# A state-space and feed-forward kernel: kernel products in steps of 48 matmuls, and an empty step behind inverse rows

## The chip, the cores and the metric

The kernel runs on one core of a Trainium2 chip. The metric is the device time in microseconds; the median of the runs shown is 1351.43 us. Beside it stands one profiled execution, which took 1350.32 us, with a span of 1348.5 us from its first to its last instruction.

## What is computed

One block with adaptive layer norm, for 2048 tokens of width 576: a state-space convolution (S4D), then a feed-forward network, both with a residual, in float32. Cut to what matters:

```python
def conv(u, ...):                        # _A_ref
    K = 2.0 * einsum("dn,dnl->dl", C, exp(A * dt * pos)).real
    y = irfft(rfft(u, 2 * L) * rfft(K, 2 * L))[:L]
    return y + u * D_skip
def ffn(x, w1, w2):                      # _B_ref, Dff = 4608
    return maximum(x @ w1, 0) @ w2

h = layernorm(x) * (1 + ca) + sa         # ca, sa, ga, ... from silu(c) @ w_mod
x = x + ga * conv(h)
h = layernorm(x) * (1 + cb) + sb
x = x + gb * ffn(h)
```

## The kernel before

The 2048 tokens are cut into four blocks of 512. The convolution is done blockwise by transforms of 1024 points that are written as matrix products and butterflies; block s needs the spectra of the inputs of all blocks up to s and those of the convolution kernel K.

K comes from products of power tables, `W2` (32 rows for each of 48 channels) and `W1`. A *head* h is 48 channels; there are twelve. For a stretch of K the tables of a head are rotated on VectorE (`rot`, lines 404 to 416: two multiplications with 1536 elements, two additions with 768), and then multiplied on TensorE (`products`, line 440): for each of 12 values q, for real and imaginary part, four 32-row matmuls that lie beside each other in the array. The result of six q, a *half* of 48 matmuls, fills the one PSUM buffer of the tag `cps`, and ScalarE copies it out (line 450). The first part of K is made before the feed-forward stage starts (`KGen`, line 262). The rest is made beside it by `rest`, with three widths: na = 48 columns (parts 1 to 3 together) and na = 16 (part 1 alone) in block 0, na = 32 (parts 2 and 3) in block 1.

The feed-forward stage fills most of the time. For each of 4 x 36 *groups* g of 128 hidden columns, `first(g)` makes 14 matmuls into `hps` (line 1326; float32 as a sum of high and low parts `xh`, `xl`, `xs`), ScalarE writes `hh` (line 1331) and VectorE `hl` (line 1332) out of it, and `second(g - 2)` makes 14 more into five accumulators `acc` (line 1351). There are two `hps` buffers. The weights `w` are loaded, split on ScalarE (lines 1297, 1304) and VectorE, and their low parts kept in HBM for the later blocks.

While block s is in the feed-forward stage, the *side work* for block s + 1 is woven in. It is a chain of Python generators (`gens`): in block 0 `rest` for the heads 0 to 5, then convolution 1; in block 1 the output of block 0 (`finish`), `rest` for the heads 6 to 11, then convolution 2; in block 2 convolution 3. Four times in each group `step` takes pieces from the chain. A piece of VectorE work yields its estimated microseconds; a piece of TensorE work yields `None`, which counts one of at most two such pieces for this step and 0.7 of credit; -1 ends the step. A step goes on while the credit is under its target, a rate times the step's number:

```python
            while done[0] < target and v < min(room, 2.7) and pe < 2:
                w = next(gen, 0)
                if gen.gi_frame is None or w == -1:
                    return
                if w is None:
                    pe += 1
                    done[0] += 0.7
```

At a block's end the rest of its chain is emitted at once. `spread` puts one yield of the products behind each rotation operation (behind each second one at na = 32, each third at na = 48). A recording layer then fixes each engine's order, so the order on an engine is not quite the order in which the code was emitted.

At the end of a convolution `inverse` makes four rows of tokens for each half of the channels: two matmuls into a `cps` buffer (line 1019), a yield of `None`, an addition to the residual x on VectorE (recorded by the helper `v`, line 510), a yield of 0.45. In blocks 1 to 3 there is one `cps` buffer, so a row's matmuls need the previous row's addition. Then follow the statistics of the next norm (`norm2`, BN_AGGR at line 819, the square root on ScalarE at line 820) and transposes (line 1070) into `xh`, `xl`, `xs` for the next block.

Of the kernel before, what the change touches and what calls it, by code (L numbers as in the profile page):

```python
# [46 lines left out]
class KGen:  # L47
# [335 lines left out]
    def rest(self, psum, items, beside=iter(())):  # L383
# [6 lines left out]
        with ExitStack() as ctx:  # L390
# [37 lines left out]
            def products(h, W1, W2, blocks):  # L428
                na = 16 * len(blocks)
                key = (h // 6, blocks)  # L430
                if key not in kes:
                    kes[key] = pt.tile([P, na, 72], F32, name=f"ker_{h}")
                ke = kes[key]
                for half in range(2):
                    ps = psum.tile([P, 6, na], F32, tag="cps", bufs=1, name="kps")
                    for q in range(6):
                        for r in range(2):
                            for dd in range(4):
                                ch = dd * 12 + 6 * half + q
                                nc.tensor.matmul(  # L440
                                    ps[32 * dd : 32 * dd + 32, q, :],
                                    W2[:, r, :, ch],
                                    W1[:, :na, r, ch],
                                    start=(r == 0),
                                    stop=(r == 1),
                                )
                        if q == 2:
                            yield None
                    q0 = 12 * (h % 6) + 6 * half
                    nc.scalar.activation(  # L450
                        ke[:, :, q0 : q0 + 6], ps.rearrange("p q a -> p a q"), AF.Copy
                    )
                    yield None
                rows[key] = rows.get(key, 0) + 1
                if rows[key] == 6:
                    yield -1
                    for i, s in enumerate(blocks):
                        self.store(
                            s, h // 6, ke[:, 16 * i : 16 * i + 16].rearrange("p a q -> p (a q)"),
                            nc.gpsimd,  # L460
                        )
# [5 lines left out]
            for i, (h, blocks) in enumerate(items):  # L467
                W2, W0, Z = nxt
                W1 = pt.tile([P, most, 2, H], F32, tag="W1", bufs=2, name=f"W1r_{h}")
                yield from spread(rots(W1, W0, Z, blocks), prev, len(blocks))  # L470
                if i + 1 < len(items):
                    nxt = load(items[i + 1][0])
                prev = products(h, W1, W2, blocks)
                if i + 2 == len(items):
                    yield next(beside, -1)
# [12 lines left out]
class Body:  # L488
# [381 lines left out]
    def conv(self, s):  # L870
# [4 lines left out]
        x2 = self.x2p[s % 2].tile([P, 4, D], F32, tag="x2", bufs=1, name=f"x2_{s}")  # L875
# [70 lines left out]

        def inverse(p, V):
            ops = lambda n2: [(self.gc[:, n2, c, :], V[:, n2, c]) for c in range(2)]
            return self.inverse(x2, p, ops)

        def back(p, Y):
            V = self.spec(f"V_{s}_{p}")
# [16 lines left out]
        else:  # L969
# [10 lines left out]
            yield from product(0, Y)  # L980
        yield from back(0, Y)
        yield from both(spec_K(1, ZK), after(3, inverse(0, Vs[0])))
        Y = self.spec(f"Y_{s}_1")
        yield from product(1, Y)
        yield from back(1, Y)
        yield -1
        yield -1
        yield from inverse(1, Vs[1])
        yield from self.norm2(s, x2, xp)

# [18 lines left out]
            v(y, y, T, op=op or ALU.add)  # L1009
            yield 1.35  # L1010

    def inverse(self, x2, p, ops, order=(0, 2, 1, 3)):

        xv = x2.rearrange("m n (dd p q) -> m n dd p q", dd=4, p=2)
        for n2 in order:
            ps = self.cps.tile([P, 512], F32, tag="cps", bufs=self.nps, name="ps_i")
            todo = ops(n2)
            for i, (a, b) in enumerate(todo):
                self.nc.tensor.matmul(  # L1019
                    ps[:, :PC], a, b, start=(i == 0), stop=(i == len(todo) - 1)  # L1020
                )
            yield None
            pv = ps[:, :PC].rearrange("m (dd q) -> m dd q", dd=4)
            self.v(xv[:, n2, :, p], pv, xv[:, n2, :, p], op=ALU.add)
            yield 0.45

    def norm2(self, s, x2, xp, st=None):

# [553 lines left out]
```

## Time and profile before

| | us |
|---|---|
| median of the runs | 1351.43 |
| fastest run | 1349.67 |
| profiled execution | 1350.32 |
| its span | 1348.5 |
| first to last FF matmul | 214.8 to 1342 |

Busy time by stage of this execution (the four blocks of the feed-forward stage begin at 214.8, 550.0, 846 and 1108 us):

| stretch, us | PE busy | DVE busy | ACT busy | PE clock | GB/s |
|---|---|---|---|---|---|
| 214.8 to 550 | 324.9 of 335.2 | 291.1 | 102.2 | 0.97 | 291 |
| 550 to 846 | 291.5 of 296.0 | 206.9 | 104.2 | 0.99 | 283 |
| 846 to 1107.8 | 261.1 of 261.8 | 163.1 | 96.1 | 1.00 | 247 |
| 1107.8 to 1342 | 234.2 of 234.2 | 30.2 | 69.9 | 1.00 | 177 |

How to read the lines: PE is TensorE, PEld its weight loads, DVE VectorE, ACT ScalarE, POOL GpSimd, SP SyncE. A row of the order in time gives the start in us, the busy time, engine, line, operation, tiles out<-in, and the number of merged instructions; in brackets stands the idle time before it and what ended it, "issue" where the profile shows nothing that was waited for. Matmuls overlap, so PE's busy time says little of how fast they follow each other: for that the starts are compared. A float32 product of line 440 or 1019 appears as two matmul records, an FF matmul or a transpose as one.

### The profile page before, as it was taken

What the parts mean: (1) busy time and instruction counts of PE and PEld (TensorE: products, weight loads), DVE (VectorE), ACT (ScalarE), POOL (GpSimd) and SP (SyncE); (2) the same over time, 40 slices, a digit from 0 to 9 for tenths busy, and PEclk for the clock granted to TensorE, in tenths of its full rate; (3) what the DMA queues carried; (4) which work ended last, traced back from release to release, by engine and by line L of the source; (5) the groups of instructions that cost most, each with busy time, mean ns of one, the idle gap of its engine ahead of it and who ended that gap; (6) DMA issues with size and microseconds to landing.
All of it is one profiled execution on the core that took longest, in us unless ns stands there. A gap on an engine that the chain in (4) does not pass through costs nothing. (4 is left out here: it accounts for less than half of the span.)

```text
span 1348.5 us, 26042 instructions
## 1 busy us (share of the span) xinstructions
PE 1227.2 (91%) x10608; PEld 974.3 (72%) x10608; DVE 870.4 (65%) x1351; ACT 504.1 (37%) x1014; POOL 195.6 (15%) x271
## 2 busy tenths in 40 slices
PE   5124798999999998999999899999999999999998
PEld 3123566777777787787777787787888888888886
DVE  5977998999886899379546976376989221111111
ACT  7986234222224322622233225343222353332321
POOL 1777331111121100111101000100010000000000
PEclk9555898999999998999999999999999999999999
DMA  6666399888798975699688895767997556666651
GB/s 197 239 254 230 110 366 376 329 297 297 264 340 278 328 266 183 213 395 338 228 280 302 289 351 162 247 187 260 321 345 239 175 178 217 194 197 201 194 170 62
DMA packets 132424, 340.47 MB, mean 252 GB/s; under 512 B 22352, under 2 KB 22672, under 8 KB 132304
## 3 DMA queue, kind: packets, MB, share of 16 engines
q1 hardware_dynamic: 105200, 215.21, 48.1%
q0 software_dynamic: 26816, 123.01, 25.0%
q8 instruction: 83, 1.36, 0.4%
q10 hardware_dynamic: 288, 0.59, 0.1%
q14 instruction: 37, 0.30, 0.1%
HBM read 258.55 MB, written 80.22 MB: 251 GB/s over the span
## 5 line engine op out<-in xcount | busy, mean ns | idle before, releaser
L1351 PE MATMUL acc<-hh,w 128*128 128x512 f32 x1296 | 422.6, 400 | 2.1 <-DVE w L510 2.0
L1326 PE MATMUL hps<-xh,w 128*128 128x512 f32 x1152 | 395.9, 404 | 1.2 <-ACT xh L1082 1.2
L1351 PEld LDWEIGHTS acc<-hh,w 128*128 128x128 f32 x1296 | 243.8, 189 | 55.6 <-DVE w L510 2.8
L1351 PE MATMUL acc<-hl,w 128*128 128x512 f32 x720 | 279.9, 399 | 0.0
L1332 DVE SCALAR_TENSOR_TENSOR hl<-hps,hh 128x512 fp32r<-128x512 f32 x144 | 99.3, 689 | 279.8 <-ACT hh L1331 279.6
L1326 PEld LDWEIGHTS hps<-xh,w 128*128 128x128 f32 x1152 | 217.2, 190 | 49.7 <-ACT xh L1082 3.3
L1326 PE MATMUL hps<-xl,w 128*128 128x512 f32 x576 | 231.1, 401 | 0.6 <-DVE xl L1087 0.6
L1331 ACT ACTIVATE hh<-hps 128x512 fp32r<-128x512 f32 x144 | 86.2, 598 | 343.9 <-PE hps L1326 335.7
L1304 ACT ACTIVATE w<-r 128x576 fp32r<-128x576 f32 x144 | 98.7, 686 | 237.3 <-issue 183.9
L1351 PEld LDWEIGHTS acc<-hl,w 128*128 128x128 f32 x720 | 135.8, 189 | 28.3
L1326 PEld LDWEIGHTS hps<-xl,w 128*128 128x128 f32 x576 | 109.2, 190 | 25.6 <-DVE xl L1087 2.2
L262 PE MATMUL kps<-W,W 128*32 128x16 f32 x2304 | 40.1, 218 | 74.4 <-POOL W L59 49.3
L1297 ACT ACTIVATE w<-r 128x640 fp32r<-128x640 f32 x142 | 103.9, 732 | 5.9 <-DMA r<-in_w_dram 5.9
L1326 PE MATMUL hps<-xs,w 128*128 128x512 f32 x288 | 98.2, 421 | 2.9 <-DVE hl L1332 2.7
L262 PEld LDWEIGHTS kps<-W,W 128*32 128x32 f32 x2304 | 37.7, 150 | 79.1 <-POOL W L59 50.7
L510 DVE TENSOR_TENSOR Y<-Y,T 128x1152 f32<-128x1152 f32 x64 | 85.0, 1356 | 0.1
L440 PEld LDWEIGHTS kps<-W1r,W2r 128*32 128x32 f32 x3456 | 64.4, 146 | 26.8 <-issue 20.2
L440 PE MATMUL kps<-W1r,W2r 128*32 128x48 f32 (+2 forms) x3456 | 73.4, 238 | 3.9 <-issue 3.9
L759 ACT ACTIVATE Z<-ps_f 128x288 f32<-128x288 f32 x104 | 42.4, 408 | 63.9 <-PE ps_f L758 62.9
L1326 PEld LDWEIGHTS hps<-xs,w 128*128 128x128 f32 x288 | 53.6, 192 | 16.0 <-DVE hl L1332 4.2
L510 DVE TENSOR_TENSOR W<-Z 128x576 f32<-128x576 f32 x52 | 37.1, 756 | 40.9 <-ACT Z L759 40.9
L510 DVE TENSOR_TENSOR w<-r,w 128x512 fp32r<-128x512 f32 (+2 forms) x108 | 58.4, 580 | 3.0 <-ACT w L1304 3.0
(216 smaller groups left out, 1370.1 us busy)
## 6 DMA issues: line engine op xcount, KB each, us to landing
r<-in_w_dram SPq DMA_DIRECT2D x144, 320.0 KB, 4.3
r<-in_w_dram SPq DMA_DIRECT2D x144, 288.0 KB, 3.9
w<-L1d SPq DMA_DIRECT2D x108, 320.0 KB, 3.0
w<-L2d SPq DMA_DIRECT2D x108, 288.0 KB, 3.1
W2r<-W2d POOLq DMA_DIRECT2D x18, 1536.0 KB, 10.0
W2d<-W SPq DMA_DIRECT2D x10, 1536.0 KB, 7.4
W<-W1d POOLq DMA_DIRECT2D x18, 768.0 KB, 9.1
Ua<-Ud POOLq DMA_DIRECT2D x12, 1152.0 KB, 10.0
```

What stands on the lines that cost most here:

```text
L262: self.nc.tensor.matmul(ps[32 * dd : 32 * dd + 32, 12 * u + q, :], W2[:, r, :, ch], W1[:, u, :, r, ch], start=(r == 0), stop=(r == 1),)
L440: nc.tensor.matmul(ps[32 * dd : 32 * dd + 32, q, :], W2[:, r, :, ch], W1[:, :na, r, ch], start=(r == 0), stop=(r == 1),)
L510: return self.kept(self.nc.vector.tensor_tensor(*args, **kw))
L759: nc.scalar.activation(Z[:, n2, c], ps[:, :PC], AF.Copy)
L1297: nc.scalar.activation(w[:, 0], r, AF.Copy)
L1304: nc.scalar.activation(w[:, 0:D], r2[g], AF.Copy)
L1326: nc.tensor.matmul(ps, a, x, start=(i == 0), stop=(i == 13))
L1331: nc.scalar.activation(hh, ps, AF.Relu)
L1332: nc.vector.scalar_tensor_tensor(hl, ps, 0.0, hh, op0=ALU.max, op1=ALU.subtract)
L1351: nc.tensor.matmul(acc[i], a, x, start=(f == 0 and j in (0, 3, 6, 9, 12)), stop=(f == NF - 1 and j in (2, 5, 8, 11, 13)),)
```

## The change

Two edits. In `products` the yield behind the third q of a half stays only at na = 48. At 16 and 32 columns a half is then one TensorE piece of 48 matmuls with 0.7 of credit, where it was two pieces of 24 with 1.4. In the convolutions 2 and 3 (s > 1) each row of `inverse` yields -1 behind its addition, which ends the step.

```diff
@@ -444,7 +444,7 @@
                                     stop=(r == 1),
                                 )
-                        if q == 2:
+                        if q == 2 and na == 48:
                             yield None
@@ -946,7 +946,7 @@
         def inverse(p, V):
             ops = lambda n2: [(self.gc[:, n2, c, :], V[:, n2, c]) for c in range(2)]
-            return self.inverse(x2, p, ops)
+            return self.inverse(x2, p, ops, spaced=s > 1)
@@ -1009,7 +1009,7 @@
-    def inverse(self, x2, p, ops, order=(0, 2, 1, 3)):
+    def inverse(self, x2, p, ops, order=(0, 2, 1, 3), spaced=False):
@@ -1023,6 +1023,8 @@
             self.v(xv[:, n2, :, p], pv, xv[:, n2, :, p], op=ALU.add)
             yield 0.45
+            if spaced:
+                yield -1
```

Lines behind 1023 stand two further on in the changed kernel (1326 is 1328 there). Both edits move the side work behind them, since the credit of a step decides how much of the chain the next one takes.

How the change moves instructions is shown at three places. On ScalarE, beside the last products of 32 columns in block 1 (`ker` is the copied half of K, `mv` the statistics of the next norm, `hh` and `w` the FF stage's), before:

```order
L450 ACTIVATE ker_6735<-kps 128x32x6
L820 ACTIVATE mv<-mv,eps 128x1 x4
L1304 ACTIVATE w_7329<-r_7072 128x576
L450 ACTIVATE ker_6735<-kps 128x32x6
L1331 ACTIVATE hh<-hps 128x512
L1297 ACTIVATE w_7354<-r_7325 128x640
```

and in the change:

```order
L1306 ACTIVATE w_7437<-r_7222 128x576
L820 ACTIVATE mv<-mv,eps 128x1 x2
L1333 ACTIVATE hh<-hps 128x512
L1299 ACTIVATE w_7460<-r_7433 128x640
L450 ACTIVATE ker_6735<-kps 128x32x6
L820 ACTIVATE mv<-mv,eps 128x1 x2
L450 ACTIVATE ker_6735<-kps 128x32x6
```

The four roots are two pairs now, and an eviction of products stands behind the first pair, with hh and a weight split between. On TensorE, the first products of 32 columns in block 1, before:

```order
L440 MATMUL kps<-W1r_6628,W2r_6566 32x32 x48
L1351 MATMUL acc_36_6515<-hh,w_6603 128x512 x2
L1351 MATMUL acc_36_6515<-hl,w_6603 128x512
L1351 MATMUL acc_36_6516<-hh,w_6603 128x512 x2
L1351 MATMUL acc_36_6516<-hl,w_6603 128x512
```

and in the change:

```order
L440 MATMUL kps<-W1r_6628,W2r_6566 32x32 x48
L1353 MATMUL acc_36_6515<-hh,w_6603 128x512 x2
L440 MATMUL kps<-W1r_6628,W2r_6566 32x32 x48
L1353 MATMUL acc_36_6515<-hl,w_6603 128x512
L1353 MATMUL acc_36_6516<-hh,w_6603 128x512 x2
```

The second half of the head follows behind two FF matmuls, where before its first 24 products came 14 FF matmuls after. On TensorE, the first inverse rows of convolution 2 in the change (those of before stand in the prediction):

```order
L1019 MATMUL ps_i<-V_0_8456,gc 128x288 x2
L1328 MATMUL hps<-xs_6142,w_8418 128x512 x2
L1328 MATMUL hps<-xh_6140,w_8418 128x512
L1328 MATMUL hps<-xl_6141,w_8418 128x512
L1328 MATMUL hps<-xh_6140,w_8418 128x512 x2
L1328 MATMUL hps<-xl_6141,w_8418 128x512
L1328 MATMUL hps<-xh_6140,w_8418 128x512 x2
L1328 MATMUL hps<-xl_6141,w_8418 128x512
L1328 MATMUL hps<-xh_6140,w_8418 128x512 x2
L1328 MATMUL hps<-xl_6141,w_8418 128x512
L1328 MATMUL hps<-xh_6140,w_8418 128x512
L1019 MATMUL ps_i<-V_0_8456,gc 128x288 x2
```

Fourteen FF matmuls lie between the first row and the second.

## Prediction

> **What bounds the kernel now.** I read the page first, then the busy time by stretches, then the order in time around groups of side work.
>
> ```profile
> span 1348.5 us, 26042 instructions
> PE 1227.2 (91%) x10608; PEld 974.3 (72%) x10608; DVE 870.4 (65%) x1351; ACT 504.1 (37%) x1014; POOL 195.6 (15%) x271
> q8 instruction: 83, 1.36, 0.4%
> L440 PE MATMUL kps<-W1r,W2r 128*32 128x48 f32 (+2 forms) x3456 | 73.4, 238 | 3.9 <-issue 3.9
> 1200.00:1300.00 100.00, 100.00 (x443) 82.81 (x442) 11.07 (x16) 30.62 (x48) 0.00 (x0) 1.00 0.64 196
> ```
>
> From 214.8 us to 1342 us TensorE hardly rests. Where it has feed-forward (FF) matmuls almost alone (the stretch row), 443 start in 100 us, 0.226 us each. So in these 1127 us everything else that PE does, and every wait of PE, adds to the end; the other engines count only where they make PE wait. Each convolution matmul has two records in the trace (1728 products of line 440 stand as 3456 records).
>
> **Part 1, fewer groups.** What does a cut in the products cost? Here is a step of 24 products (48 records) and one of two steps in a row:
>
> ```profile
> 599.79 0.39 PE L1326 MATMUL hps<-xh,w 128*128 128x512 f32 x1
> 600.11 0.94 PE L440 MATMUL kps<-W1r,W2r 128*32 128x32 f32 x48
> 600.98 0.73 PE L1351 MATMUL acc<-hh,w 128*128 128x512 f32 x2
> 601.55 0.39 PE L1351 MATMUL acc<-hl,w 128*128 128x512 f32 x1
> ...
> 631.57 0.39 PE L1351 MATMUL acc<-hl,w 128*128 128x512 f32 x1
> 631.89 1.65 PE L440 MATMUL kps<-W1r,W2r 128*32 128x32 f32 x96
> 633.47 0.72 PE L1326 MATMUL hps<-xs,w 128*128 128x512 f32 x2
> 634.03 0.40 PE L1326 MATMUL hps<-xh,w 128*128 128x512 f32 x1
> ```
>
> From FF matmul to FF matmul the 24 take 600.98 - 599.79 = 1.19 us, less 0.226 for the matmul itself 0.96, and the two matmuls behind take 0.57 instead of 0.45: 1.08 us. The 48 take 1.67 + 0.11 = 1.78 us. Two 24s cost 2.16, so a cut costs 0.38 us. In PE's order the groups of line 440 beside FF matmuls fall from 63 to 46 (32 columns 21 to 12, 16 columns 24 to 18, 48 columns 18 to 16): 17 x 0.38 = **-6.4 us**, the widths taken alike.
>
> **Part 2, what denser groups meet.** In the kernel-generation stage TensorE runs products without FF matmuls:
>
> ```profile
> 109.34 2.15 PE L262 MATMUL kps<-W,W 128*32 128x16 f32 x127 [1.42 <-issue]
> 113.30 2.15 PE L262 MATMUL kps<-W,W 128*32 128x16 f32 x128 [1.81 <-issue]
> 117.14 2.14 PE L262 MATMUL kps<-W,W 128*32 128x16 f32 x128 [1.70 <-issue]
> ```
>
> Runs of 127 or 128 records, each behind a wait for nothing that the profile shows. With their weight loads 128 records are 256 instructions, and the page has 83 packets on the instruction queue for PE's 2 x 10608: one packet per 256. I read the waits as the arrival of the next block of instructions. Blocks start 3.96 and 3.84 us apart though they run in 2.15. Beside FF matmuls (a block of them alone runs 128 x 0.226 = 29 us) this is hidden, except in two places, of which this is one:
>
> ```profile
> 252.83 1.51 PE L440 MATMUL kps<-W1r,W2r 128*32 128x16 f32 x88
> 254.27 0.73 PE L1326 MATMUL hps<-xs,w 128*128 128x512 f32 x2
> 254.93 0.90 PE L440 MATMUL kps<-W1r,W2r 128*32 128x16 f32 x48
> ...
> 257.12 0.54 PE L440 MATMUL kps<-W1r,W2r 128*32 128x16 f32 x20
> 259.44 0.66 PE L440 MATMUL kps<-W1r,W2r 128*32 128x16 f32 x28 [1.78 <-issue]
> 260.02 0.81 PE L1326 MATMUL hps<-xh,w 128*128 128x512 f32 x2
> ...
> 263.61 0.79 PE L1351 MATMUL acc<-hh,w 128*128 128x512 f32 x2
> 348.15 0.52 PE L440 MATMUL kps<-W1r,W2r 128*32 128x16 f32 x19 [1.65 <-issue]
> 259.40:348.10 88.70, 86.54 (x1405) 68.26 (x1405) 82.61 (x87) 21.18 (x39) 12.07 (x18) 0.98 0.86 297
> ```
>
> Between the two waits lie 1405 matmuls and as many weight loads, 2810 instructions, and 11 x 256 is 2816: both fall on a block's end (six waiting instructions are not counted as records). Counting 128 records back from 257.66, the block began near 253.4: it ran 4.2 us and waited 1.78, a turnaround of 6.0. Behind the wait nine FF matmuls take 263.61 - 260.02 = 3.59 us where 2.03 would do, at half speed: 1.6 us more. The two stalls cost 1.78 + 1.65 + 2 x 1.6 = 6.6 us.
>
> The change moves them. PE at the first stall, before (names: kps is the products' PSUM tile, hps and acc the two FF ones):
>
> ```order
> L440 MATMUL kps<-W1r_3032,W2r_3026 32x16 x44
> L1326 MATMUL hps<-xs_2779,w_3024 128x512 x2
> L440 MATMUL kps<-W1r_3032,W2r_3026 32x16 x24
> L1326 MATMUL hps<-xh_2777,w_3024 128x512
> L1326 MATMUL hps<-xl_2778,w_3024 128x512
> L1326 MATMUL hps<-xh_2777,w_3024 128x512 x2
> L1326 MATMUL hps<-xl_2778,w_3024 128x512
> L440 MATMUL kps<-W1r_3032,W2r_3026 32x16 x24
> ```
>
> and in the change:
>
> ```order
> L440 MATMUL kps<-W1r_3032,W2r_3026 32x16 x44
> L1328 MATMUL hps<-xs_2779,w_3024 128x512 x2
> L440 MATMUL kps<-W1r_3032,W2r_3026 32x16 x48
> L1328 MATMUL hps<-xh_2777,w_3024 128x512
> L1328 MATMUL hps<-xl_2778,w_3024 128x512
> ```
>
> Now 44 and 48 products with two FF matmuls between, 186 records. Eight such pairs stand in PE's order: six at 16 columns, two at 32. Counted from the known block ends, in five of them (the first, fourth and sixth at 16 columns, both at 32) one block begins and ends inside the pair. Such a block runs 126/96 x 1.65 + 0.66 (from 254.27 to 254.93) = 2.8 us. Against a turnaround of 3.8 to 6.0 the wait is 1.0 to 3.2 us; I take 2.1, the middle, and half of the 1.6 for the slow clock, since some waits are short: 5 x 2.9 = 14.5, less the 6.6 that go: **+7.9 us**. Bounds: -6.6 with no wait at all, and 5 x 4.8 = +24 with the long turnaround and the old two kept.
>
> [...]
>
> **Part 3, the empty step.** One inverse row waits long for VectorE:
>
> ```profile
> 765.80 1.13 PE L1019 MATMUL ps_i<-V,gc 128*128 128x288 f32 x4
> 766.55 0.84 PE L1326 MATMUL hps<-xh,w 128*128 128x512 f32 x2
> ...
> 768.85 0.40 PE L1351 MATMUL acc<-hl,w 128*128 128x512 f32 x1
> 773.24 2.29 PE L1019 MATMUL ps_i<-V,gc 128*128 128x288 f32 x4 [3.99 <-DVE x L510]
> 774.91 1.47 PE L1351 MATMUL acc<-hh,w 128*128 128x512 f32 x2
> ...
> 779.50 0.39 PE L1351 MATMUL acc<-hl,w 128*128 128x512 f32 x1
> 766.64 1.43 DVE L510 TENSOR_TENSOR W<-Z 128x576 f32<-128x576 f32 x2
> 772.72 0.46 DVE L510 TENSOR_TENSOR x<-ps_i,x 128x288 f32<-128x288 f32 x1
> ```
>
> The second row needs the PSUM buffer that the first one's add frees, and that add stands behind 6.1 us of VectorE work (766.64 to 772.72). From 768.85 to 779.50 eleven FF matmuls and one row (0.75) should take 3.2 us and take 10.65: 7.4 us lost, wait and slow clock. In PE's order the second row stands ten FF matmuls behind the first:
>
> ```order
> L1019 MATMUL ps_i<-V_0_8469,gc 128x288 x2
> L1326 MATMUL hps<-xh_6187,w_8415 128x512 x2
> L1326 MATMUL hps<-xl_6188,w_8415 128x512
> L1326 MATMUL hps<-xh_6187,w_8415 128x512 x2
> L1326 MATMUL hps<-xl_6188,w_8415 128x512
> L1326 MATMUL hps<-xh_6187,w_8415 128x512
> L1351 MATMUL acc_36_6515<-hh,w_8441 128x512 x2
> L1351 MATMUL acc_36_6515<-hl,w_8441 128x512
> L1019 MATMUL ps_i<-V_0_8469,gc 128x288 x2
> ```
>
> In the change 14 lie between them, 14 to the third, 7 to the fourth (before 10, 12 and 3), and on VectorE the first add comes before one FF eviction (hl) that it used to follow. Four matmuls are 0.9 us; with the earlier add I expect 1.4 of the 4.0 to stay, and some slow clock. Bounds: 0.9 and 7.4; I take **-5 us**. The other rows of convolutions 2 and 3 wait little and gain nothing. The empty step issues nothing itself.
>
> **Part 4, the neighbours.** With half the credit per product, block 0's chain runs ahead: its last transposes stand 20 to 26 FF matmuls earlier, and 1.2 us of waiting at the block's end goes, **-1.1 us**. In block 1 two square roots of the next norm now stand on ScalarE before the eviction of an earlier half, at 32 columns:
>
> ```order
> L820 ACTIVATE mv<-mv,eps 128x1 x2
> L1333 ACTIVATE hh<-hps 128x512
> L1299 ACTIVATE w_7460<-r_7433 128x640
> L450 ACTIVATE ker_6735<-kps 128x32x6
> ```
>
> Before, all four roots stood with an eviction both ahead and behind, and PE did not wait. Now the roots wait for BN_AGGR on VectorE, behind hl and two adds; behind the roots stand an FF eviction (hh), a weight split (w) and the half's eviction (ker), and the next 48 products wait for that one, seven FF matmuls later.
>
> ```profile
> PE hps L1326 <- ACT xh L1082: 1.2, 2, 0.7
> ACT mv L820 <- DVE mv L819: 16.4, 7, 3.4
> L1332 DVE SCALAR_TENSOR_TENSOR hl<-hps,hh 128x512 fp32r<-128x512 f32 x144 | 99.3, 689 | 279.8 <-ACT hh L1331 279.6
> L414 DVE TENSOR_TENSOR W1r<-W1r,T 128x768 f32<-128x768 f32 x36 | 34.4, 956 | 0.0
> L1331 ACT ACTIVATE hh<-hps 128x512 fp32r<-128x512 f32 x144 | 86.2, 598 | 343.9 <-PE hps L1326 335.7
> L1297 ACT ACTIVATE w<-r 128x640 fp32r<-128x640 f32 x142 | 103.9, 732 | 5.9 <-DMA r<-in_w_dram 5.9
> L450 ACT ACTIVATE ker<-kps 128x192 f32<-128x192 f32 x12 | 4.1, 340 | 11.4 <-PE kps L440 11.3
> ```
>
> If VectorE is at hl when the half ends: 0.69 + 2 x 0.96 there, then 0.60 + 0.73 + 0.34 on ScalarE, 4.3 us without the small aggregates and roots; 7 x 0.226 = 1.6 cover it, 2.7 are left, and 1.6 more if the clock halves. With VectorE further on it is 0, so the bounds are 0 and 4.3; I take **+3 us**, nearer the upper, since that state needs no luck.
>
> **Sum.** -6.4 + 7.9 - 5 - 1.1 + 3 = -1.6 us on the profiled execution (span 1348.5, its time 1350.3, 1.1 below the median 1351.4): **1349 us**.
>
> **Rivals.** (a) *The instruction blocks stay hidden*: no wait inside the eight pairs. For it: only two such waits in the 42 groups at 16 and 48 columns before. Then -6.4 - 6.6 - 5 - 1.1 + 3 = -16, **1334 us**. [...] Chance 0.20. (b) *The block ends decide, slower*: with turnarounds near 6.0, as at 257 us, five waits of 3.2 + 1.6 are 24; less 3.3 for one of the old two: +20.7 - 6.4 - 5 - 1.1 + 3 = +11, **1362 us**. It outweighs the rest once the mean turnaround passes 5 us. Against it: the generation stage turned around in 3.9. Chance 0.27. (c) *The empty step doesn't do what it says*: VectorE stays equally late, row two still waits 3.1 us with the slow clock: +4 on my sum, **1353 us**, chance 0.08. My forecast has 0.45.
>
> **How the numbers follow.** A measurement of this kernel tells about 2%, 27 us, from no change. All cases lie inside that: all gains and no loss give 1329, all losses about 1371. Faster 0.02, same 0.95, slower 0.03. The range leaves one tenth out on each side: 1335 to 1364 us.
>
> **What would show it.** Right: 46 groups at line 440; waits marked issue of 1 to 3 us inside the close pairs, at 16 columns near 256, 345 and 400 us, at 32 near 590 and 660; the 4.0 us wait for x gone or under 2; a PE wait for the eviction near 645 us. Wrong: no issue waits (a), or block 1's rows still waiting as long (c).

## The result, and the profile after

| | before | after |
|---|---|---|
| median of 12 runs, us | 1350.11 | 1356.56 |
| lowest, us | 1346.77 | 1352.73 |
| profiled execution and its span, us | 1350.32, 1348.5 | 1361.79, 1360.0 |

The changed kernel takes 1.0054 times as long, 95% interval 1.0040 to 1.0068: 6.4 us more, where 2 us less had been forecast. That is inside the 2% that count as no change, but the sign is wrong and the interval leaves no doubt of it. The median lies inside the forecast's range of 1335 to 1364 us, midway between the forecast and rival (b). One of the twelve runs of the kernel before took 1761.53 us and does not enter the ratio. The profiled execution of the change was the longest of its twelve, 5.2 us above the median; that has to be kept in mind below.

From the page of the changed kernel:

```profile
q8 instruction: 83, 1.36, 0.4%
L440 PE MATMUL kps<-W1r,W2r 128*32 128x48 f32 (+2 forms) x3456 | 71.1, 237 | 17.6 <-issue 17.6
```

and from its waits of TensorE (us in total, times, longest):

```profile
PE kps L262 <- issue: 27.0, 13, 3.8
PE kps L440 <- issue: 17.6, 8, 4.5
PE hps L1328 <- ACT xh L1084: 2.3, 1, 2.3
PE ps_i L1019 <- DVE V L510: 2.1, 1, 2.1
PE ps_i L1019 <- DVE x L510: 0.3, 1, 0.3
```

Two rows of the same view before:

```profile
PE ps_i L1019 <- DVE x L510: 4.6, 2, 4.0
PE ps_i L1019 <- DVE V L510: 1.0, 1, 1.0
```

The same matmuls are there (3456 records at line 440, 83 blocks of instructions), a little less busy, and the idle time ahead of them has gone from 3.9 to 17.6 us, all of it marked issue. The wait of the inverse rows for x has gone from 4.6 to 0.3 us; they wait 2.1 us for V once, 1.0 before. The order in time shows where the issue waits lie, first in the close pairs at 16 columns, then in one at 32:

```profile
255.47 1.50 PE L440 MATMUL kps<-W1r,W2r 128*32 128x16 f32 x88
256.90 0.73 PE L1328 MATMUL hps<-xs,w 128*128 128x512 f32 x2
257.56 1.27 PE L440 MATMUL kps<-W1r,W2r 128*32 128x16 f32 x73
261.80 0.55 PE L440 MATMUL kps<-W1r,W2r 128*32 128x16 f32 x23 [2.96 <-issue]
262.28 0.80 PE L1328 MATMUL hps<-xh,w 128*128 128x512 f32 x1
...
267.56 0.47 PE L1353 MATMUL acc<-hh,w 128*128 128x512 f32 x1
...
344.06 0.74 PE L440 MATMUL kps<-W1r,W2r 128*32 128x16 f32 x34 [1.79 <-issue]
344.74 0.50 PE L1328 MATMUL hps<-xl,w 128*128 128x512 f32 x1
345.07 0.40 PE L1328 MATMUL hps<-xh,w 128*128 128x512 f32 x1
345.40 1.62 PE L440 MATMUL kps<-W1r,W2r 128*32 128x16 f32 x92
349.43 0.31 PE L440 MATMUL kps<-W1r,W2r 128*32 128x16 f32 x4 [2.41 <-issue]
...
411.89 0.68 PE L440 MATMUL kps<-W1r,W2r 128*32 128x16 f32 x32 [4.50 <-issue]
...
604.53 1.65 PE L440 MATMUL kps<-W1r,W2r 128*32 128x32 f32 x96
606.11 0.73 PE L1353 MATMUL acc<-hh,w 128*128 128x512 f32 x2
606.77 1.56 PE L440 MATMUL kps<-W1r,W2r 128*32 128x32 f32 x89
611.33 0.33 PE L440 MATMUL kps<-W1r,W2r 128*32 128x32 f32 x7 [3.00 <-issue]
```

The second group of a pair stops in the middle, after 73 and 89 of its 96 records in the two that are shown whole. Behind its first 16 records a group has read both parts of both of its tables and holds its buffer, so nothing that it could still wait for is made by another engine. Counted 128 records back, the block that ran out at 261.80 had begun 53 records before the end of the first group, at 256.0: 5.8 us from block to block. At 611.33 it is 5.9 us (from 605.4); counted in the same way the six waits of over 1 us give 5.4 to 7.4, the two short ones (0.17 us at 651.50, 0.86 at 677.06) 4.3 and 3.8. From wait to wait there are 1277, 128, 255, 639, 1018, 638 and 511 matmul records, each a multiple of 128 less 0 to 6. And behind the first wait the clock is slow: from 262.28 to 267.56 the granted clock is 0.50, and twelve FF matmuls take 5.28 us, 0.44 each, where 442 take 100 us from 1200 to 1300 us, 0.226 each.

The trace also has the packets of the instruction queue one by one: 83 of 16384 bytes, which is 64 bytes for each of 256 instructions. Each of the eight waits ends 1.3 to 1.6 us after one of them has landed: the packet of 259.39 has landed at 260.48 and TensorE goes on at 261.80, that of 409.58 at 410.47 (411.89), that of 608.69 at 609.72 (611.33). So what TensorE waits for can be seen: its next instructions.

Where the time went, stretch by stretch. The FF matmuls are the same 4032 in every version, so their numbers serve as milestones; each entry is the time from the start of one to the start of the other, in the profiled execution (before, number 104 starts at 250.21 and number 560 at 413.64):

| FF matmuls | 0-104 | 104-560 | 560-1008 | 1008-1160 | 1160-1440 | 1440-2016 |
|---|---|---|---|---|---|---|
| what lies beside them | 48 and 16 col. | 48 and 16 col. | convolution 1 | block 1 begins | 32 col. | convolution 2 |
| before | 35.4 | 163.4 | 136.4 | 40.3 | 89.1 | 166.6 |
| after | 36.3 | 177.3 | 135.8 | 38.0 | 94.5 | 159.4 |
| products_only | 35.6 | 171.9 | 135.5 | 37.9 | 94.7 | 160.2 |
| empty_only | 36.7 | 164.3 | 136.4 | 40.3 | 92.5 | 164.5 |
| c16_only | 36.5 | 172.1 | 135.4 | 38.0 | 90.4 | 166.1 |
| c32_only | 36.6 | 166.9 | 136.0 | 40.2 | 94.6 | 160.8 |
| gap2_halves | 36.6 | 163.1 | 139.1 | 40.3 | 86.1 | 169.6 |
| shift128 | 37.7 | 173.4 | 135.3 | 37.9 | 98.8 | 162.0 |
| c32_gap | 35.7 | 164.9 | 136.5 | 40.3 | 86.3 | 163.0 |
| c32_gap_n | 36.0 | 161.7 | 136.1 | 40.3 | 86.0 | 159.7 |
| c32_gap16 | 36.1 | 168.4 | 137.1 | 40.6 | 90.8 | 161.1 |

After against before: +13.9 in the stretch of 48 and 16 columns, +5.4 in that of 32, -7.2 in convolution 2, -2.9 about the end of block 0, +0.9 in the first stretch, 1.8 by a later start of the FF stage, and -0.4 behind number 2016: 11.5 us, the difference of the two spans. Three other executions with the same order in the second stretch took 171.9 to 173.4 us there, so 177.3 is on the high side.

### The profile page after: what moved, and what is told of

It reads as the page before. It is cut to its first block, busy times and chain, and to the rows that moved or that the text cites. A ratio compares the mean times of both kernels' runs of the same rounds, so it can differ in the third digit from the quotient of the medians.

```text
span 1360.0 us, 26042 instructions
## 1 busy us (share of the span) xinstructions
PE 1224.2 (90%) x10608; PEld 975.5 (72%) x10608; DVE 871.0 (64%) x1351; ACT 504.9 (37%) x1014; POOL 193.8 (14%) x271
## 4 chain that ended last, share of the span: by engine, by line
PE 72%; DVE 14%; DMA 6%; issue 5%; ACT 2%; POOL 1%; SPq 0%; DVEq 0%; ACTq 0%; POOLq 0%
PE hps L1328 29%; PE acc L1353 28%; PE kps L440 5%; PE ps_f L758 4%; DVE T L510 3%; DVE Y L510 3%; PE kps L262 2%; DVE W L510 2%; DMA Ua<-Ud 2%; DMA Ud<-U 1%; PE kps L607 1%; PE ps_i L1019 1%; DMA W1d<-W 1%; DVE k L133 1%; ACT c L56 1%
## 5 line engine op out<-in xcount | busy, mean ns | idle before, releaser
L1333 ACT ACTIVATE hh<-hps 128x512 fp32r<-128x512 f32 x144 | 86.1, 598 | 330.0 <-PE hps L1328 322.8
L262 PE MATMUL kps<-W,W 128*32 128x16 f32 x2304 | 40.2, 218 | 76.9 <-POOL W L59 49.9
L440 PEld LDWEIGHTS kps<-W1r,W2r 128*32 128x32 f32 x3456 | 63.5, 146 | 35.6 <-issue 26.1
L440 PE MATMUL kps<-W1r,W2r 128*32 128x48 f32 (+2 forms) x3456 | 71.1, 237 | 17.6 <-issue 17.6
L510 DVE TENSOR_TENSOR w<-r,w 128x640 fp32r<-128x640 f32 (+2 forms) x108 | 58.3, 579 | 7.1 <-ACT w L1306 6.8
```

The source lines that it names most:

```text
L262: self.nc.tensor.matmul(ps[32 * dd : 32 * dd + 32, 12 * u + q, :], W2[:, r, :, ch], W1[:, u, :, r, ch], start=(r == 0), stop=(r == 1),)
L440: nc.tensor.matmul(ps[32 * dd : 32 * dd + 32, q, :], W2[:, r, :, ch], W1[:, :na, r, ch], start=(r == 0), stop=(r == 1),)
L510: return self.kept(self.nc.vector.tensor_tensor(*args, **kw))
L1333: nc.scalar.activation(hh, ps, AF.Relu)
```

## The experiments

Three theories stood at the start. The *block theory*: TensorE waits for the arrival of its next 256 instructions, so the place of a wait is set by the count of instructions, and its size by how long a block takes to arrive. The *buffer theory*: the second half of a pair waits for ScalarE to empty the one PSUM buffer, which the profile doesn't show. The *order theory*: the loss comes from side work that the edits shift, not from these waits. Medians and ratios to the kernel before, of interleaved runs; each kernel ran beside the kernel before on one chip:

| kernel | median, us | ratio, 95% | issue waits of the products, us (times) |
|---|---|---|---|
| after | 1356.56 | 1.0054 (1.0040 to 1.0068) | 17.6 (8) |
| products_only | 1357.8 | 1.0048 (1.0030 to 1.0067) | 15.1 (7) |
| empty_only | 1349.72 | 0.9991 (0.9977 to 1.0006) | 5.9 (3) |
| gap2_halves | 1357.87 | 1.0055 (1.0035 to 1.0076) | 5.6 (4) |
| shift128 | 1375.79 | 1.0180 (1.0152 to 1.0208) | 17.8 (7) |
| c16_only | 1356.2 | 1.0047 (1.0027 to 1.0067) | 12.0 (6) |
| c32_only | 1353.27 | 1.0022 (1.0001 to 1.0042) | 10.9 (5) |
| c32_gap | 1346.55 | 0.9967 (0.9948 to 0.9985) | 5.5 (4) |
| c32_gap_n | 1344.91 | 0.9955 (0.9935 to 0.9976) | 3.7 (3) |
| c32_gap16 | 1350.48 | 0.9989 (0.9966 to 1.0013) | 11.3 (7) |

### products_only and empty_only: which edit loses

```diff
-            return self.inverse(x2, p, ops, spaced=s > 1)
+            return self.inverse(x2, p, ops, spaced=False)
```

> The products in steps of 48 without the empty step. Block theory (a close pair of groups swallows a whole block of 256 instructions, and TensorE then waits for the next block): the order of the close pairs is that of the changed kernel, so eight waits of 16 to 18 us in sum on the products' line, marked issue, at the same places, and without the empty step's gain of about 5 us the time is 1358 to 1363 us, 6 to 12 above before. Rival 'the loss comes from the empty step or from what it moves in convolutions 2 and 3': the products alone then are a gain, 1343 to 1349 us. Rival 'PSUM buffer' (the waits are for ScalarE's eviction of the half before): as the block theory in time.

```diff
-                        if q == 2 and na == 48:
+                        if q == 2:
```

> The empty step without the products in steps of 48. Block theory: the two issue waits of before (1.8 and 1.7 us) and no more on the products' line; the wait for x of 4.0 us at the first inverse rows gone or under 2.5; 1343 to 1348 us, 3 to 7 below before. Rival 'the empty step loses': 1352 us or more.

The products alone give 1357.8 us, the whole loss (just under the 1358 to 1363 expected, with seven waits of 15.1 us instead of eight of 16 to 18); the empty step alone 1349.72, no change that can be told (between 0.2% less and 0.1% more). So the products lose, as the block theory has it, and the empty step is not what moves the time. It doesn't bring the 3 to 7 us that were expected of it either. Of its three issue waits the two of before are 2.2 and 2.4 us; the third, 1.27 us at 604.05, is of another kind, which shift128 shows below. Its wait for x is there at 2.4 us; with the products alone the second row follows 2.82 us behind the first and waits for nothing. empty_only:

```profile
769.10 1.13 PE L1019 MATMUL ps_i<-V,gc 128*128 128x288 f32 x4
775.87 2.23 PE L1019 MATMUL ps_i<-V,gc 128*128 128x288 f32 x4 [2.42 <-DVE x L510]
```

products_only:

```profile
771.63 1.13 PE L1019 MATMUL ps_i<-V,gc 128*128 128x288 f32 x4
774.45 1.13 PE L1019 MATMUL ps_i<-V,gc 128*128 128x288 f32 x4
```

What removed the stall of the inverse rows in the changed kernel is thus the first edit, not the second (160.2 in that stretch with the products alone, 164.5 with the empty step alone, 166.6 before).

### shift128: do the waits go by the count of instructions?

```diff
+                    for _ in range(self.again(r)):      # 32 times in all
+                        self.nc.tensor.matmul(..., W2[:, r, :, ch], W1[:, u, :, r, ch],
+                                              start=True, stop=True)
```

> The changed kernel with 32 more products in the kernel generation before the feed-forward stage (a product that is made anyway is made 32 times more, and overwritten: nothing of the result changes), which are 128 more instructions of TensorE: every block end behind them moves by half a block, 64 matmuls, and no order or wait behind them changes. They cost 1 to 4 us themselves. Block theory: the waits inside the close pairs move. Counted by the order, the shortest blocks then lie in the second, third and fifth pair of 16 columns and none under 3.7 us lies in the pairs of 32 columns: waits of 1.5 to 4 us near 281, 310 and 375 us, and those at 257, 345 and 406 us (first, fourth and sixth pair) and at 606 and 674 us (32 columns) gone or under 1 us; sum 8 to 13 us instead of 17.6. PSUM-buffer and order rivals: all waits stay where they were, at 257, 345, 406, 606 and 674 us plus 1 to 4, sum 16 to 18.

Nothing in TensorE's order behind the added products changes, only the count. In its order in time (line 456 is 440, 1369 is 1353):

```profile
268.59 1.63 PE L456 MATMUL kps<-W1r,W2r 128*32 128x16 f32 x96
270.15 0.50 PE L1344 MATMUL hps<-xh,w 128*128 128x512 f32 x1
...
295.62 1.09 PE L456 MATMUL kps<-W1r,W2r 128*32 128x16 f32 x60
300.84 0.79 PE L456 MATMUL kps<-W1r,W2r 128*32 128x16 f32 x36 [4.13 <-issue]
...
334.35 1.42 PE L1369 MATMUL acc<-hh,w 128*128 128x512 f32 x5 [1.41 <-issue]
```

The first pair, which waited 2.96 us in the changed kernel, runs through. The second pair, which had not waited, now waits 4.13 us. At the third 1.41 us are waited in front of an FF matmul, which needs nothing of the products' buffer. The fifth waits, the sixth doesn't, and both pairs of 32 columns that had waited (FF matmuls 1164 and 1360) run through, while two other groups there wait (0.6 and 1.8 us, at 1253 and 1288). The moves were foretold from the count alone, with two misses: the fourth pair, expected free, still waits (2.0 and 2.3 us), and the wait of 1.8 us beside 32 columns was not expected. Counted from the start of the program, the waits of the fourth pair stand at records 4429 and 4557, as they do in the changed kernel, and those ahead of and behind them whole blocks away (3663, 4174, 5068): the work has moved by 64 records, the places of the waits have not. The buffer theory can't move a wait without moving an instruction of the pair; it falls, and so does the order theory as to where the waits lie.

One of its seven waits, though, is of another kind. It stands in front of a group, not inside it (PE, and VectorE beside it):

```profile
626.74 0.34 PE L456 MATMUL kps<-W1r,W2r 128*32 128x32 f32 x8 [4.20 <-issue]
624.00 1.76 DVE L426 TENSOR_TENSOR W1r<-W,Zr 128x1536 f32<-128x1536 f32 x1 [2.45 <-DMA W<-W1d]
625.68 0.95 DVE L428 TENSOR_TENSOR W1r<-W1r,T 128x768 f32<-128x768 f32 x1
```

The group starts 0.1 us after VectorE has made the real part of its table (625.68 + 0.95), which was late because the load of the table before it was: the word issue hides a chain from DMA over VectorE. The packets tell the two kinds apart: ahead of 626.74 the last one had landed 8.6 us before. The wait of empty_only at 604.05 is of this kind too, 0.1 us behind the real part of its table. Without the 4.2 us 13.6 are left, against 8 to 13 expected; blocks that ran 4.0 us wait too (ahead of 648.69 and 662.75). The 128 instructions cost far more than the 1 to 4 us put down for them: the FF stage starts 9.6 us later (226.15 against 216.57).

### gap2_halves: take the pairs apart

```diff
+                    if na < 48:
+                        yield -1
+                        yield -1
```

> The changed kernel, with the step ended behind each half of 16 or 32 columns and one empty step behind it, so that no block of 256 instructions runs in less than 3.7 us by the order; groups of products 48 instead of 46. Block theory: the eight issue waits of 1.4 to 4 us go, at most three small ones of under 1 us stay, sum under 3 us instead of 17.6, and little slow clock behind them: 1336 to 1344 us, below both kernels. PSUM-buffer rival: the halves are further apart, so the waits go too and the time is the same (not told apart here). Rival 'order' (the loss comes from TensorE's work being drawn together and not from the waits): 1350 us or more.

Its waits of TensorE:

```profile
PE kps L440 <- issue: 5.6, 4, 2.0
PE ps_i L1022 <- DVE x L513: 3.8, 1, 3.8
PE ps_t L1075 <- ACT h L1064: 3.5, 5, 1.3
```

The cause and its place are confirmed: with the halves two steps apart the issue waits fall from 17.6 to 5.6 us (not to the 3 expected: two of the four are 2.0 us), the stretch of 16 columns takes 163.1 us instead of 177.3, that of 32 columns 86.1 instead of 94.5. The time doesn't follow: 1357.87, against 1336 to 1344 expected, and 1350 or more was the forecast of the order theory. The price stands in the other columns and rows: the side work is later by the empty steps, so the end of block 0 has 5.6 us more (139.1 and 40.3 against 135.8 and 38.0, with a wait of 2.8 us for hl at 533 and 2.1 us of waits about its last transposes), and convolution 2 10.2 us more (169.6 against 159.4: its second inverse row waits 3.8 us for x again, and 4.9 us are waited at the block's end, from 844 to 850, for the norm and its transposes), and block 2 has 4.3 more up to FF matmul 2600 (159.0 against 154.7). So the order theory is right about one thing: where the side work stands is worth about as much at the ends of the blocks as the waits are, and giving the freed credit back loses that.

### c16_only and c32_only: which width

```diff
-                        if q == 2 and na == 48:
+                        if q == 2 and na != 16:         # c16_only
+                        if q == 2 and na != 32:         # c32_only
```

> Steps of 48 products at 16 columns alone (with the empty step). Block theory: TensorE's order in block 0 is that of the changed kernel, so the waits near 257, 341, 345, 368 and 406 us are all there, and the stretch from FF matmul 104 to 560 takes 171 to 178 us (before 163.4, changed kernel 177.3); none of over 1 us at 32 columns. Time 1356 to 1365 us. Rival 'the loss is in block 1, where the work is drawn together': 1347 to 1352 us.

> Steps of 48 products at 32 columns alone (with the empty step). Block theory: block 0 as before (163 to 165 us from FF matmul 104 to 560), one wait of 2 to 4 us in each of the two close pairs of 32 columns (FF matmuls 1164 and 1360), block 1 slower there by 5 us; but the inverse rows stand where they stand in the changed kernel, whose block 1 lost nothing at them, so in sum 1343 to 1349 us, 2 to 7 below before. Rival 'the loss is in block 1': 1355 us or more.

At 16 columns alone: 1356.2 us, 172.1 in the second stretch, both as expected (the waits at 608 us beside 32 columns are 0.5 us each). At 32 columns alone, the stretch is as expected (94.6), convolution 2 is as in the changed kernel (160.8), and yet it takes 1353.27 us, not 1343 to 1349. Block 0, whose order is that of before, took 166.9 us where the same order took 161.7 to 164.9 in four other executions: its own three issue waits came out longer (6.7 us against 3.9 before). So 16 columns lose by themselves. At 32 the stretch loses 5.5 us and convolution 2 gains 5.8, and what is left of a loss, 1.0001 to 1.0042, lies in this profile ahead of FF matmul 560, where the order is that of before: that 32 columns alone lose time is not shown.

### c32_gap, c32_gap_n and c32_gap16: a version that beats both

c32_gap keeps 16 columns as before and puts the merged halves of 32 one step apart; c32_gap_n has no empty step in the inverse; c32_gap16 ends the step behind halves of 16 columns as well.

```diff
-                        if q == 2 and na == 48:
+                        if q == 2 and na in (48, 16):
...
+                    if na == 32:
+                        yield -1
```

> As c32_only, with the step ended behind each half of 32 columns, so that no two halves are close. Block theory: no wait of over 1 us marked issue at 32 columns, and the stretch from FF matmul 1160 to 1440 takes 85 to 87 us (before 89.1, changed kernel 94.5): the nine groups fewer at 0.38 us show as a gain. Time 1340 to 1346 us if the inverse rows of convolution 2, which stand 28 FF matmuls later than in c32_only, find VectorE in time; up to 1350 us if they don't. Rival 'order': 89 us or more in that stretch.

> As c32_gap without the empty step of the inverse rows. What is the empty step worth in the kernel that is faster? If it is what keeps the inverse rows of convolution 2 from waiting (theory of the prediction): a wait of 2 to 4 us for x at the first rows, 1349 to 1353 us. If it is the place of the rows, 21 FF matmuls later than before, that does it: no such wait, 1344 to 1349 us as with the step (1346.6).

> As c32_gap, and the step ended behind each half of 16 columns too (these stay steps of 24). By the order the shortest blocks of block 0 are still 3.8 us long, but two fewer of under 4.6 us, and six groups fewer stand at 16 columns. Block theory: two of the three waits on the products' line in block 0 stay or move, the stretch from FF matmul 104 to 560 takes 160 to 164 us (164.9 in c32_gap) and the whole 1342 to 1347 us. If later work of block 0 is pushed into its end, as with the wider spacing (3.1 us more there), the gain goes: 1347 to 1351 us.

c32_gap is 0.9967 of before (0.9948 to 0.9985), c32_gap_n 0.9955 (0.9935 to 0.9976): faster than both kernels, by less than the 2% that count as a change, and not to be told from each other. In the stretch of 32 columns they take 86.3 and 86.0 us against 89.1 before, with no issue wait of over 0.4 us. Waits of c32_gap_n:

```profile
PE kps L440 <- issue: 3.7, 3, 2.2
PE ps_i L1021 <- DVE V L512: 0.6, 2, 0.4
```

No inverse row waits for x, though there is no empty step: the 1349 to 1353 us expected if the step did it are excluded. c32_gap16 did not come out as forecast: 168.4 us in the second stretch instead of 160 to 164, where its more even order still waits four times for 1.2 to 2.3 us, and 90.8 us in that of 32 columns, where TensorE's order is that of c32_gap and should have given 86. There the largest wait is again one of VectorE's:

```profile
613.76 0.35 PE L440 MATMUL kps<-W1r,W2r 128*32 128x32 f32 x8 [2.63 <-issue]
611.03 1.76 DVE L410 TENSOR_TENSOR W1r<-W,Zr 128x1536 f32<-128x1536 f32 x1 [2.18 <-DMA W<-W1d]
```

The load of a table landed 2.18 us too late for VectorE, and the products behind it paid; the last packet of instructions had landed 4.8 us before 613.76.

### dma_gen: what makes a block late

```diff
+            for u in range(2):
+                if g < 4:
+                    nc.sync.dma_start(out=k.XX[2 * g + u], in_=k.W2d[2 * g + u])
```

> The changed kernel with eight more copies in the kernel generation: each of the first eight W2 tables, just stored in HBM, is copied once more to a place in HBM that nothing reads (1.5 MB read and written each). It asks whether a block of instructions arrives later when the DMA engines are busy. In the changed kernel the products' waits on line 262 are 27.0 us in 13 (23.4, 23.1 and 21.9 in three others), blocks start 3.5 to 4.0 us apart where only products run, DMA share 0.56; in the feed-forward stage 5.3 to 7.4 us apart at a share of 0.8 to 0.9. If the load decides: with the share over 0.8 beside the products these waits come to 33 us or more, and blocks 4.5 to 6 us apart. If the stage decides for another reason: 22 to 28 us as without the copies, 3.5 to 4.2 us apart. The time of the whole is of no interest.

The waits, the order in time of the kernel generation, and the DMA share beside it (last figure but one of a stretch):

```profile
PE kps L262 <- issue: 40.3, 13, 5.4
```

```profile
75.05 2.15 PE L262 MATMUL kps<-W,W 128*32 128x16 f32 x127 [4.74 <-issue]
81.08 2.14 PE L262 MATMUL kps<-W,W 128*32 128x16 f32 x128 [3.88 <-issue]
...
130.19 2.14 PE L262 MATMUL kps<-W,W 128*32 128x16 f32 x128 [2.24 <-issue]
133.92 2.14 PE L262 MATMUL kps<-W,W 128*32 128x16 f32 x127 [1.59 <-issue]
141.49 1.72 PE L262 MATMUL kps<-W,W 128*32 128x16 f32 x99 [5.42 <-issue]
```

```profile
66.00:92.00 26.00, 10.26 (x607) 9.71 (x606) 13.16 (x31) 12.27 (x22) 17.92 (x26) 0.55 0.95 345
127.00:136.00 9.00, 5.17 (x316) 4.91 (x310) 3.75 (x9) 3.94 (x8) 7.75 (x15) 0.50 0.60 226
136.00:142.00 6.00, 0.58 (x38) 0.51 (x36) 0.01 (x1) 0.00 (x0) 2.94 (x4) 0.50 0.98 338
```

and the changed kernel in the same stage and in block 0:

```profile
60.00:90.00 30.00, 13.22 (x768) 12.46 (x768) 21.99 (x52) 23.90 (x58) 27.63 (x35) 0.50 0.53 200
250.00:430.00 180.00, 166.45 (x2674) 132.79 (x2673) 151.91 (x183) 41.17 (x80) 27.00 (x41) 0.93 0.83 294
```

The same products, the same 13 waits: 40.3 us instead of 27.0 (and 21.9 to 27.6 in the other versions that add nothing there). Where the copies keep the DMA engines at 0.95, 81.08 starts 6.0 us after 75.05 (the starts from 68.18 to 90.08 us lie 6.9, 6.0, 4.0 and 5.0 us apart); in the lull at 0.60, 133.92 starts 3.7 us after 130.19; at 0.98 the next wait is 5.4 us. So in this execution a block mostly arrived later when the DMA engines were busier. The packets show where the time goes: one takes 0.9 to 1.8 us with the copies or without, and TensorE goes on 1.2 to 1.6 us after it has landed; what grows is the time until it starts, 3.7 of the 6.0 us from 75.05 and 1.3 of the 3.7 us from 130.19. What holds it up was not shown, and this is a single execution. This is what the forecast lacked.

## Why the prediction was wrong

**The step that failed is the size of the term of part 2, +7.9 us.** The mechanism was right, down to the place: five waits were forecast, in the first, fourth and sixth pair at 16 columns and in both at 32, and all five are there, ending at 261.80, 349.43, 411.89, 611.33 and 677.06 us. Three things were too small.

- *The turnaround.* I took the middle of 3.8 to 6.0 us, so 5 x 2.1 = 10.5 us of waits. But 3.8 came from the kernel generation, at a DMA share of 0.53; beside the products of 16 columns the share is 0.83, and the five turnarounds are 3.8 to 7.4, with waits of 13.7 us. The short one, 3.8 at 677.06, falls into a lull of the DMA engines (0.54 from 673.2 to 677.06). Rival (b) had used 6.0, and put 1362 us; the median, 1356.6, lies midway.
- *The number of waits.* Only blocks that lie wholly inside a pair were counted, with 2.8 us of run time. With 6 us to arrive, longer blocks wait too: 1.79 us at 344.06, 1.89 at 372.52, and 0.2 at a third place, 3.9 us that were put at nothing. (The kernel before, too, had a third such wait, 0.5 us at 280.60, which the prediction left out.)
- *The slow clock.* I put 0.8 us for each wait, 4.0 in all, and this is the largest miss. In the two stretches of products 51 FF matmuls follow the one before at over 0.38 us, 16 before the change: 11.0 us lost against 3.2.

In sum, from the rows of this execution: 17.6 - 3.9 = 13.7 of waits and 7.8 of slow clock, **+21.5 instead of +7.9**. In products_only, nearer to the median, 15.1 - 3.9 + 8.8 - 3.2 = +16.8. The two stretches grew by 13.9 + 5.4 = 19.3 us: these 21.5, and 2.5 of seven matmul groups of line 758 that stood behind the stretches before and stand in them now, less 4.7 by the fewer groups of products.

**Part 1, -6.4 us, holds nearly.** c32_gap and c32_gap_n, with the nine cuts at 32 columns and next to no wait, gain 2.8 and 3.1 us there, about 0.3 us a cut where 0.38 was reckoned: -5.6 for 17; in the changed kernel itself 4.7 are left, by the sum above.

**Part 3, -5 us, was right in size and wrong in cause.** Convolution 2 takes 7.2 us less; 1.4 of it is four groups of line 758 that stand ahead of it now, which leaves 5.8 of the 7.4 that the stall cost. But products_only, which has no empty step, gains 6.4 (5.0 beside the same four groups), and c32_gap_n, which has none either, 6.9, though 12 of its transposes now stand behind FF matmul 2016, where block 2 takes 1.8 us more up to number 2600 (156.5 against 154.7). The empty step alone gains 2.1. That the size came out is luck. In the changed kernel the first row starts shortly before its addition (PE and VectorE):

```profile
780.79 1.13 PE L1019 MATMUL ps_i<-V,gc 128*128 128x288 f32 x4
782.58 0.46 DVE L510 TENSOR_TENSOR x<-ps_i,x 128x288 f32<-128x288 f32 x1
```

From the row to its addition it is 1.8 us, where it was 6.9 before (765.80 to 772.72): VectorE is further ahead of TensorE. I had let the first addition come earlier by one FF eviction alone, and for the rest let the empty step stretch the distance between the rows. What gives VectorE the lead (TensorE's own waits at 32 columns, or the rows' later place in c32_gap_n) was not separated.

**Part 4.** The end of block 0 gave 2.9 us, not 1.1, though part of it is side work that now stands earlier (three groups of line 758, 0.3 us each), and the wait for xh rose from 1.2 to 2.3. The +3 us for the roots on ScalarE did not come at all:

```profile
662.46 1.67 PE L440 MATMUL kps<-W1r,W2r 128*32 128x32 f32 x96
...
665.89 1.66 PE L440 MATMUL kps<-W1r,W2r 128*32 128x32 f32 x96
```

The second group follows after seven FF matmuls with no idle time. I had said that the bad state needs no luck; it needed VectorE to be late, and the aggregates came at 662.60, while the first of these groups still ran.

**Rivals.** (a), blocks stay hidden: excluded by 17.6 us of waits. (b), block ends decide: what happened, milder in the median because convolution 2 and the end of block 0 gave back 10 us where it had counted 6, and the 3 us on ScalarE did not come. (c), the empty step does nothing: true of the empty step, and without effect on the sum, since the products did its work.

## What to carry to other kernels

An edit that saves TensorE time by packing many short matmuls together must be counted in instructions as well as in us: here blocks of 256 that ran in 2.8 to 4.5 us, beside DMA engines at a mean share of 0.83 (250 to 430 us), ran TensorE dry, and a stretch of long matmuls between the packed groups repaid that (c32_gap, 86.3 us against 94.5 in its stretch). A time to arrive is to be taken from a stage with the same DMA load, not from the stage where it is easiest to see: in dma_gen blocks started 3.7 us apart at a share of 0.60 and 4.0 to 6.9 at 0.95. And what a wait is worth is not the end of the account: gap2_halves removed most of the waits (5.6 us left of 17.6) and gave the gain back at the ends of the blocks.

## What the runs showed of the hardware that was not expected

Blocks of instructions came later beside much data: the same 13 waits took 27.0 us (DMA share 0.53 from 60 to 90 us) and 40.3 us with the copies (0.95 from 66 to 92 us). A wait marked issue can be checked against the packets of the instruction queue: here TensorE went on 1.3 to 1.6 us after one had landed. An addition of 128 small instructions in the kernel generation delayed the FF stage by 9.6 us. And a wait did not settle the clock directly behind it: behind 1.79 us at 344.06 the granted clock stays at 1.00 for another 2.2 us and is 0.50 from 346.22 to 353.05, so it fell before the next wait began at 347.03. Behind the 1.78 us before the change it is 0.50 from 260.56, 1.1 us after the wait's end, to 263.97; with the 2.96 us of the change it falls at 260.89, inside the wait, and stays until 267.72. These stretches last 3.4 or 6.8 us each.
